# A share of the last weight block of a decode kernel is loaded ahead by a transfer of four by eight rows

## The chip, the cores and the metric

The kernel runs on one core of a Trainium2 chip. The metric is the device time of one execution in microseconds (us); the runs shown are compared by their median. All data is float32.

## The reference

Eight tokens (one for each of eight sequences) pass through an attention block that reads a key and value cache and, beside it, through a dense block; both results are added to the input.

```python
xn = _layernorm(x)                                    # x: 8 x 512
q  = xn @ wq                                          # 32 heads of 128, wq: 512 x 4096
scores = einsum("bhqd,bhkd->bhqk", q, k) * 128 ** -0.5   # 8 kv heads, 8192 keys, 4 q heads share one
p  = softmax(scores)
o  = einsum("bhqk,bhkd->bhqd", p, v)
A  = o.reshape(8, 4096) @ wo                          # wo: 4096 x 512
B  = mish(xn @ w1 + b1) @ w2                          # w1: 512 x 1792, w2: 1792 x 512
out = x + A + B
```

The key cache and the value cache have 268 MB each; everything else together is some 24 MB. So nearly all of the time goes into moving about 561 MB from memory into the core.

## The kernel before, in words

**Tiling and stages.** The work is cut into 16 packs (`PACKS`): four pairs of kv heads (`PAIRS`) by four pairs of sequences (`NP`, `PB`). Of each pack the loop takes two halves `b`. One half's keys or values are one transfer of 8 MB to all 128 partitions (64 KB a partition). For a half, `scores` (L353) multiplies the keys by the queries in 16 steps `r` of four TensorE passes each, `rows` (L365), `maximum`, `exponents`, `fold` and `weights` make the softmax's weights, and a round later `values` (L460) multiplies them by the values; `gather` (L471, L473) and `merge` (L488, L492) leave the head outputs `oT`. After a pair of heads is complete, `turn` (L514 to L528) brings `oT` into the layout in which `wo` lies, as `oW`, by four products with a selection matrix `tid` and four copies of 32 partitions, and `outputs` multiplies it by that pair's 2 MB of `wo`. `wo` lies so that partition p holds four rows of 1024 numbers (two head halves h by 512 output columns), 16 KB in all.

**Loads.** All big loads go through one queue, that of SP (L121), in one fixed order: the list `queue`, which `plan_k`, `plan_v`, `plan_wq`, `plan_wo` and the plan of `w2` fill ahead of time. Three places in the core's memory take them: `a` (64 KB a partition), `b` (80 KB a partition, so that two key loads overlap only in part) and `w` (16 KB a partition). `pump` issues the next load of the list as soon as its place is free, and `release` says that a place is free; the issue itself then waits on SP for the last instructions that read the bytes which it overwrites. SP takes its instructions in order, so a waiting load holds back all that stand behind it.

**The tail.** Behind the last pack, the order of the list is: the values of half 0 into `b`, the values of half 1 into `a` in two parts (three quarters and one quarter), and then `w2` in four parts (two, two, two and one of seven rows of 4 KB a partition) with the two halves of the last `wo` between them, as w2 0, w2 1, wo half 0, w2 2, wo half 1, w2 3. TensorE, VectorE and GpSimd run their instructions in program order. On TensorE the tail is: `values(0)`, `sums`, `merge(p, 0)`, `add_up` (L548), four idle products `keep_busy(4)` (L639) whose result nobody reads, `values(1)` in two parts, `down` (L628) with w2 0, `merge(p, 1)`, `turn`, `down` with w2 1, `last_outputs` (L562) with wo half 0, one idle product, `down` with w2 2, one idle product, `last_outputs` with wo half 1, and `down` with w2 3. Then VectorE copies the result out of the accumulator `H` (L720) and SP stores it (L721).

Of the kernel before, what the change touches and what calls it, by code (L numbers as in the profile page):

```python
# [8 lines left out]
F32 = mybir.dt.float32  # L9
AF = mybir.ActivationFunctionType  # L10
ALU = mybir.AluOpType
AX = mybir.AxisListType

P = 128
B = 8
# [8 lines left out]
G = 4  # L24
# [3 lines left out]
BW = 1024  # L28
# [4 lines left out]
Q = P // G  # L33
# [5 lines left out]
PAIRS = HKV // 2  # L39
# [11 lines left out]
KR = DH * 2 * NB // P  # L51
# [12 lines left out]

QR = CC
OR = 4
W1R = 2 * CC * P // P
W2R = G * FT // 2 * FP // P
FAR = 1e38
# [3 lines left out]
def kernel(  # L73
# [12 lines left out]
    nc = tc.nc  # L86
# [12 lines left out]
    def rows_of(blocks):  # L99

        return blocks.rearrange("j p f -> (j p f)").rearrange("(p f) -> p f", p=P)
# [12 lines left out]
    def plan(what, at, blocks, parts=((0, 1),), lo=0):  # L114

        rows = rows_of(blocks)
        n = rows.shape[1]
        t = place[at][:, lo : lo + n]

        def load(cols):  # L120
            nc.sync.dma_start(t[:, cols], rows[:, cols])  # L121
            return t

        for first, end in parts:
            cols = slice(round(first * n), round(end * n))
            queue.append((what, at, lambda cols=cols: load(cols)))
# [24 lines left out]
    def plan_v(p, b, at, parts=((0, 1),)):  # L151
        plan(("v", p, b), at, blocks_of(v, p, b), parts)
# [1 line left out]
    def plan_wq(i):  # L154
        plan(("wq", i), "w", wq[i * CC : (i + 1) * CC])

    def plan_wo(i, parts=((0, 1),)):
        plan(("wo", i), "w", wo[i * 4 : i * 4 + 4], parts)


    plan_wq(0)
# [5 lines left out]
    for p in range(PACKS):  # L167
        for b in range(PB):
# [4 lines left out]
            if p > 0:  # L173
                plan_v(p - 1, b, "a")
    plan_v(PACKS - 1, 0, "b")
    plan_v(PACKS - 1, 1, "a", ((0, 3 / 4), (3 / 4, 1)))
    W2_PARTS = ((0, 2), (2, 4), (4, 6), (6, 7))
    for k, (lo, hi) in enumerate(W2_PARTS):
        plan("w2", "b", w2, ((lo / W2R, hi / W2R),))
        if 0 < k < 3:  # L180
            plan_wo(PAIRS - 1, (((k - 1) / 2, k / 2),))


    S = psum.tile([P, GK], F32, name="s")
# [18 lines left out]
    hsel = const.tile([P, V8], F32, name="hsel")  # L203

    isel = const.tile([P, W4], F32, name="isel")

    far = const.tile([P, KINDS], F32, name="far")

# [15 lines left out]
    def setup():  # L224
        make_identity(nc, ident)
        nc.gpsimd.memset(ones, 1.0)
        nc.vector.memset(xnT, 0.0)
        nc.vector.memset(O[0], 0.0)

        st = const.tile([B, 8], F32, name="st")  # L230

        scratch = pt.rearrange("p b c m t e h -> p (b c m t e h)")
        xc, sq = scratch[:B, :D], scratch[:B, D : 2 * D]
        nc.vector.reduce_sum(st[:, 0:1], x_sb, axis=AX.X)
        nc.vector.tensor_scalar_mul(st[:, 1:2], st[:, 0:1], 1.0 / D)
        nc.vector.tensor_scalar(xc, x_sb, st[:, 1:2], None, op0=ALU.subtract)
        nc.vector.tensor_mul(sq, xc, xc)
        nc.vector.reduce_sum(st[:, 2:3], sq, axis=AX.X)
        nc.vector.tensor_scalar(
            st[:, 3:4], st[:, 2:3], 1.0 / D, EPS, op0=ALU.mult, op1=ALU.add  # L240
        )
        nc.scalar.activation(st[:, 4:5], st[:, 3:4], AF.Sqrt)
        nc.vector.reciprocal(st[:, 5:6], st[:, 4:5])

        nc.vector.tensor_mul(st[:, 6:7], st[:, 5:6], st[:, 5:6])
        nc.vector.tensor_mul(st[:, 7:8], st[:, 6:7], st[:, 3:4])
        nc.vector.tensor_scalar(st[:, 6:7], st[:, 7:8], -0.5, 1.5, op0=ALU.mult, op1=ALU.add)
        nc.vector.tensor_mul(st[:, 4:5], st[:, 6:7], st[:, 5:6])
        nc.vector.tensor_scalar(xc, xc, st[:, 4:5], None, op0=ALU.mult)
        for r in range(QR):  # L250
            nc.tensor.transpose(M[:, r * B : (r + 1) * B], xc[:, r::QR], ident[:B, :B])
        nc.vector.tensor_copy(
            xnT[:, :, :, :B],
            M[:, : QR * B]
            .rearrange("p (r o b) -> p r o b", r=QR, o=1)
            .to_broadcast([P, QR, 2, B]),
        )

        wide = scratch[:B, 2 * D : 2 * D + W1R * P]
        for t in range(2):  # L260
            nc.gpsimd.tensor_copy(
                wide.rearrange("b (r c t i) -> b r c t i", r=W1R, c=CC, t=2)[:, :, :, t, :],
                xc.rearrange("b (c i r) -> b r c i", c=CC, r=W1R),
            )

        nc.vector.tensor_copy(
            gsel, ident[:G, :G].rearrange("p (g o) -> p g o", o=1).to_broadcast([G, G, B])
        )
        nc.vector.reduce_sum(bsel, ident.rearrange("p (u i) -> p u i", u=KN), axis=AX.X)
        nc.vector.reduce_sum(  # L270
            half, ident.rearrange("p (g t i) -> p t g i", g=G, t=2), axis=AX.XY
        )
        nc.vector.reduce_sum(rsel, ident.rearrange("p (g r) -> p r g", g=G), axis=AX.X)
        nc.vector.reduce_sum(hsel, rsel.rearrange("p (i r) -> p r i", i=W4), axis=AX.X)
        nc.vector.reduce_sum(isel, rsel.rearrange("p (i r) -> p i r", i=W4), axis=AX.X)
        nc.vector.tensor_scalar(far, isel, FAR, -FAR, op0=ALU.mult, op1=ALU.add)
        of_head = const.tile([P, 2, V8], F32, name="of_head")
        nc.vector.reduce_sum(
            of_head, ident.rearrange("p (e j r) -> p e r j", e=2, j=NB), axis=AX.X
        )  # L280
        nc.vector.tensor_copy(tsel, of_head.rearrange("p e (b h) -> p b e h", b=PB))
        nc.vector.memset(csel, 0.0)
        for c in range(2):
            rows = slice(HE * c, HE * (c + 1))
            for b in range(PB):
                nc.vector.tensor_copy(
                    csel[rows, b, :, b], ident[rows, rows].rearrange("p (u h) -> p u h", u=KN)
                )
        return wide
# [155 lines left out]
    def sums(p, lsel):  # L445
        n = PB * 2 * REP
        nc.tensor.matmul(M[:, 136 : 136 + n], ones, lsel, start=True, stop=True)
        RT[p] = work.tile([P, PB, 2, REP], F32, name="r")
        nc.vector.reciprocal(RT[p].rearrange("p b e h -> p (b e h)"), M[:, 136 : 136 + n])
# [45 lines left out]
                RT.pop(p).rearrange("p b e h -> p (e h) b"),  # L495
            )

    def turning():

        tid = work.tile([P, HT * KINDS * P], F32, name="e", bufs=1)[:, : OR * P]  # L500
        tid = tid.rearrange("p (r g i) -> p r g i", r=OR, g=G)
        nc.vector.tensor_copy(
            tid, ident.rearrange("p (i r o) -> p r o i", r=OR, o=1).to_broadcast([P, OR, G, Q])
        )
        return tid

    def turn(i, tid):


        to = oW[i] = work.tile([P, OR, 2, B], F32, name="oW")  # L510
        o = oT.pop(i).rearrange("p n h b -> p (n h b)")
        cols = 2 * REP * B
        for r in range(OR):
            nc.tensor.matmul(  # L514
                M[:, 256 + r * cols : 256 + (r + 1) * cols],
                tid[:, r].rearrange("p g i -> p (g i)"),
                o,
                start=True,
                stop=True,
            )  # L520
        m = M[:, 256 : 256 + OR * cols].rearrange("p (r j q) -> p j r q", r=OR, j=G)
        for j in range(G):
            rows = slice(Q * j, Q * (j + 1))
            dst = to[rows].rearrange("p r h b -> p r (h b)")
            if i == PAIRS - 1 and j % 2:
                nc.scalar.copy(dst, m[rows, j])
            else:
                nc.vector.tensor_copy(dst, m[rows, j])  # L528
# [24 lines left out]
                stop=False,  # L553
            )

    def last_outputs(lo, hi, w):

        for r in range(lo, hi):
            for h in range(2):
                for g in range(G):  # L560
                    at = r * BW + h * D + g * P
                    nc.tensor.matmul(  # L562
                        H[Q * g : Q * g + B, :P],
                        oW[PAIRS - 1][:, r, h, :],
                        w[:, at : at + P],
                        start=False,
                        stop=False,
                    )
# [67 lines left out]
    def keep_busy(n):  # L636

        for k in range(n):
            nc.tensor.matmul(C[0][:Q, :], ones[:, :Q], acc, start=True, stop=True)  # L639
# [54 lines left out]

    p = PACKS - 1
    merges()
    tid = turning()
    values(0, landed["v", p, 0])
    gather(p, 0)
    release(("v", p, 0))  # L700
    sums(p, lsel.pop(p))
    merge(p, 0)
    add_up()
    keep_busy(4)
    values(1, landed["v", p, 1], 0, ROUNDS * 3 // 4)
    values(1, landed["v", p, 1], ROUNDS * 3 // 4)
    gather(p, 1)
    w2_sb, wo_sb = landed["w2"], landed["wo", PAIRS - 1]
    down(*W2_PARTS[0], w2_sb)
    merge(p, 1)  # L710
    turn(PAIRS - 1, tid)
    down(*W2_PARTS[1], w2_sb)
    last_outputs(0, OR // 2, wo_sb)
    keep_busy(1)
    down(*W2_PARTS[2], w2_sb)
    keep_busy(1)
    last_outputs(OR // 2, OR, wo_sb)
    down(*W2_PARTS[3], w2_sb)
    res = acc[:, :P]
    nc.vector.tensor_copy(res, H[:, :P])  # L720
# [58 lines left out]
```

## Time and profile before

| what | value |
|---|---|
| median of 3 runs | 1311.45 us (1311.45 to 1311.66) |
| the profiled execution | 1311.78 us |
| its span, first to last instruction | 1310.0 us |
| TensorE busy (matmul) | 863.7 us, 66% |
| VectorE busy | 384.0 us, 29% |
| ScalarE busy | 111.7 us, 9% |
| DMA | 561.76 MB, mean 429 GB/s |
| granted TensorE clock, mean | 0.844 |

How to read the profile: a line such as "1305.18 1.06 PE L562 MATMUL h<-kvw,oW 128*8 128x128 f32 x32 [0.56 <-DMA kvw<-in_wo]" says that at 1305.18 us from the span's start TensorE began 32 matmul passes of line 562 that took 1.06 us together, and that it had sat idle for 0.56 us before until a transfer from `wo` to place `w` landed. A float32 product takes two passes. "PEld" is the weight load of a pass. In the stretches, a DMA share of 1.00 means that all 16 DMA engines were moving packets all the time.

### The profile page before, as it was taken

The numbers are of one execution on the slowest core, as the hardware profiler recorded it, in microseconds if no ns is written. First come the engines' busy times: TensorE is split into PE (matmuls) and PEld (weight loads), VectorE is DVE, ScalarE is ACT, GpSimd is POOL, SyncE is SP. The second block draws the span as 40 slices with busy tenths as digits, with TensorE's granted clock in tenths as the row PEclk, the third lists the DMA queues.
The fourth block names the chain that finished last, engine by engine and source line by source line (L and its number), as shares of the span: only waits on it lengthen the run. The fifth ranks groups of instructions, "written<-read, shape, count | busy, mean of one in ns | idle before, by whom it ended". The sixth has DMA issues, their size and how long they took to land.

```text
span 1310.0 us, 10715 instructions
## 1 busy us (share of the span) xinstructions
PE 863.7 (66%) x4776; PEld 281.5 (21%) x4776; DVE 384.0 (29%) x590; ACT 111.7 (9%) x294; POOL 4.8 (0%) x10
## 2 busy tenths in 40 slices
PE   4786556866557765677565686655875666766657
PEld 1221112212112221122111222111221221222113
DVE  7150504205051230521405032052320505114051
ACT  1020101001010100101101010010100101001010
POOL 1000000000000000000000000000000000000000
PEclk9887889878799877898878897788877879878789
DMA  9999999999999999999999999999999999999997
GB/s 404 442 423 441 433 429 430 434 437 429 438 431 431 431 439 427 439 423 441 421 444 423 419 447 431 435 427 437 423 425 434 429 439 423 439 431 435 439 425 331
DMA packets 11591, 561.76 MB, mean 429 GB/s; under 512 B 1293, under 2 KB 1425, under 8 KB 1561
## 3 DMA queue, kind: packets, MB, share of 16 engines
q1 hardware_dynamic: 11520, 561.06, 99.3%
q8 instruction: 37, 0.61, 0.2%
q14 instruction: 10, 0.07, 0.0%
q10 hardware_dynamic: 24, 0.02, 0.0%
HBM read 561.01 MB, written 0.07 MB: 428 GB/s over the span
## 4 chain that ended last, share of the span: by engine, by line
DMA 67%; PE 32%; DVE 1%; issue 0%; SPq 0%; ACT 0%; ACTq 0%
DMA kvb<-in_kT 60%; PE c L353 30%; DMA kva<-in_kT 3%; DMA kvb<-in_w 2%; DMA kvb<-in_v 2%; PE o L581 0%; PE h L312 0%; PE o L460 0%; DMA sc<-in_x 0%; SPq L121 0%; DVE nm L379 0%; PE s L365 0%; DVE qT L340 0%; PE m L293 0%; PE o L575 0%
## 5 line engine op out<-in xcount | busy, mean ns | idle before, releaser
L353 PE MATMUL c<-kvb,qT 128*64 128x512 f32 x1984 | 502.4, 671 | 347.3 <-DMA kvb<-in_kT 345.7
L353 PEld LDWEIGHTS c<-kvb,qT 128*64 128x64 f32 x1984 | 162.0, 155 | 687.6 <-issue 470.4
L460 PE MATMUL o<-kva,pt 128*32 128x512 f32 x1984 | 231.4, 620 | 24.2 <-DMA kva<-in_v 24.2
L379 DVE TENSOR_REDUCE nm<-s 128x1 f32<-128x1024 f32 x16 | 19.6, 1225 | 462.2 <-PE s L365 462.2
L412 DVE STREAM_TRANSPOSE raw<-e 128x2048 f32<-128x2048 f32 x32 | 116.0, 3626 | 14.4 <-ACT e L404 12.7
L360 ACT COPY sc<-c 128x512 f32<-128x512 f32 x32 | 18.8, 586 | 1005.0 <-PE c L353 1005.0
L460 PEld LDWEIGHTS o<-kva,pt 128*32 128x32 f32 x1984 | 65.7, 113 | 179.3 <-issue 136.2
L404 ACT ACTIVATE e<-s,nms 128x512 f32<-128x512 f32 x128 | 86.3, 686 | 126.1 <-DVE nms L393 66.8
L492 DVE TENSOR_TENSOR oT<-m,r 128x16 f32<-128x16 f32 x16 | 2.8, 175 | 229.6 <-PE m L488 229.6
L471 DVE TENSOR_SCALAR os<-o,isel 128x128 f32<-128x128 f32 x32 | 11.1, 348 | 155.4 <-PE o L460 155.4
L430 DVE TENSOR_TENSOR pt<-raw 64x256 f32<-64x256 f32 x128 | 53.6, 418 | 2.0
L365 PE MATMUL s<-sc,csel 64*128 64x512 f32 x128 | 36.1, 641 | 8.4 <-ACT sc L360 8.4
L421 DVE TENSOR_TENSOR raw<-raw 128x1024 f32<-128x1024 f32 x32 | 39.2, 1225 | 1.1
L340 DVE TENSOR_TENSOR qT<-qc,bsel 128x1024 f32<-128x1024 f32 x32 | 37.6, 1218 | 0.0
L473 DVE SCALAR_TENSOR_TENSOR os<-o,isel,os 128x128 f32<-128x128 f32 x96 | 33.7, 351 | 3.4
L404 ACT ACTIVATION_READ_ACCUMULATOR e<-s,nms 128x1 f32 x128 | 26.0, 203 | 0.0
L380 PE MATMUL m<-ident,nm 128*1 128x128 f32 x16 | 4.3, 270 | 21.2 <-DVE nm L379 21.2
L312 PE MATMUL h<-kvw,xnT 128*64 128x512 f32 x64 | 16.2, 654 | 0.0
L488 PEld LDWEIGHTS m<-hsel,os 128*128 128x128 f32 x64 | 9.5, 188 | 29.6 <-issue 23.5
L488 PE MATMUL m<-hsel,os 128*128 128x8 f32 x64 | 12.4, 266 | 4.8 <-DVE os L473 3.3
L353 PE MATMUL c<-kva,qT 128*64 128x512 f32 x64 | 14.0, 593 | 1.6 <-DMA kva<-in_kT 1.6
L323 DVE TENSOR_SCALAR e<-h 128x512 f32<-128x512 f32 x16 | 9.9, 684 | 15.9 <-PE h L312 15.9
(100 smaller groups left out, 171.4 us busy)
## 6 DMA issues: line engine op xcount, KB each, us to landing
kvw<-in_wq SPq DMA_DIRECT2D x4, 2048.0 KB, 29.7
kvw<-in_wo SPq DMA_DIRECT2D x3, 2048.0 KB, 30.7
kva<-in_v SPq DMA_DIRECT2D x1, 6144.0 KB, 27.2
kva<-in_w SPq DMA_DIRECT2D x1, 3584.0 KB, 15.8
kvb<-in_w SPq DMA_DIRECT2D x3, 1024.0 KB, 20.6
kva<-in_v SPq DMA_DIRECT2D x1, 2048.0 KB
kvw<-in_wo SPq DMA_DIRECT2D x2, 1024.0 KB, 24.6
kvb<-in_w SPq DMA_DIRECT2D x1, 512.0 KB
```

The lines of the kernel that those rows point to most:

```text
L340: nc.vector.tensor_mul(qT[:, b], qc[:, k * PB + b] .rearrange("p r (o h) -> p r o h", o=1) .to_broadcast([P, KR, KN, REP]), bsel.rearrange ...
L353: nc.tensor.matmul(C[b][HE * c : HE * (c + 1), :], t[:, r], k[:, r * BW + c * 512 : r * BW + (c + 1) * 512], start=(r == order[0]), stop=( ...
L360: nc.scalar.copy(sc, C[b])
L365: nc.tensor.matmul(S[:, c * 512 : (c + 1) * 512], csel[HE * c : HE * (c + 1), b].rearrange("p u b h -> p (u b h)"), sc[HE * c : HE * (c + ...
L379: nc.vector.tensor_reduce(nm, S, axis=AX.X, op=ALU.max, negate=True)
L404: nc.scalar.activation(ex[:, :, s, :], S[:, c * 512 : (c + 1) * 512].rearrange("p (t f) -> p t f", t=HT), AF.Exp, bias=NMS[p][:, s : s + 1 ...
L412: nc.vector.transpose(raw.rearrange("p (m t r) -> p t m r", m=TW, t=HT), ex.rearrange("p t s (q m) -> p t m (s q)", m=TW),)
L421: nc.vector.tensor_add(raw[:, :, :n], raw[:, :, :n], raw[:, :, n:])
L430: nc.vector.tensor_add(pt[rows, b, c].rearrange("p m t e h -> p (m t) e h")[:, :, e], raw[rows, :, at : at + REP], raw[rows, :, V8 + at : ...
L460: nc.tensor.matmul(O[b][Q * c : Q * (c + 1), :], pt[:, b, j % 2, j // 2].rearrange("p t e h -> p (t e h)"), vt[:, W4 * DH * j : W4 * DH * ...
L473: nc.vector.scalar_tensor_tensor(os, O[b][:, DH * i : DH * (i + 1)], isel[:, i : i + 1], os, op0=ALU.mult, op1=ALU.add,)
L488: nc.tensor.matmul(M[:, at : at + 2 * REP], OS.pop((p, b)), hsel, start=True, stop=True)
```

## The change

The last 2 MB of `wo` (`last_wo`, 128 partition rows of 16 KB) are cut in another way.

- **Far part.** The second half (8 KB, its steps r = 2 and 3) of every fourth row (rows 3, 7, 11 and so on, 32 of them, 256 KB) comes by a transfer of its own, `plan_wo_far`. It stands in the list right behind the values of half 0 and goes to partitions 0 to 31 of place `b`, behind the columns that those values take (`OX_AT`). Its source is written as four by eight rows.
- **Near part.** What is left (1792 KB) comes by three transfers into place `w`, `plan_wo_near`: the even rows whole (64 rows), rows 1, 5, 9 and so on whole (32), and rows 3, 7, 11 and so on up to their half (32). They stand together between w2 1 and w2 2; before them GpSimd clears the second half of place `w`, because the bytes that the far part left out are still multiplied, by zeros.
- **TensorE and VectorE.** `turning` makes a second selection matrix `tif` for the far rows and clears their columns in `tid`. `turn` gets two more products, into `S`, and four more VectorE instructions that pick the far part of `oW` out of them. `last_outputs` runs twice: with the far part (half of the products that the whole block takes) between w2 1 and w2 2, and with the whole near part behind it. One idle product is dropped, and four of the others are split into two and two around `merge(p, 0)` and `add_up`.

```diff
+QS = 4
+QN = P // (QS * 2 * G)
+OH = OR // 2
...
+    OX_AT = KR * BW
+    last_wo = rows_of(wo[(PAIRS - 1) * 4 :])
+    def plan_wo_far():
+        half = last_wo.shape[1] // 2
+        t = place["b"][:Q, OX_AT : OX_AT + half]
+        rows = last_wo.rearrange("(a e s) f -> s e a f", e=QN, s=QS)[QS - 1]
+        def load():
+            nc.sync.dma_start(t, rows[:, :, half:])
+            return t
+        queue.append(("wo far", "behind b", load))
+    def plan_wo_near():
+        n = last_wo.shape[1]
+        t = place["w"][:, :n]
+        what = "wo", PAIRS - 1
+        def load(first, step, cols):
+            nc.sync.dma_start(t[first::step, :cols], last_wo[first::step, :cols])
+            return t
+        queue.append((what, "w", lambda: nc.gpsimd.memset(t[:, n // 2 :], 0.0)))
+        for first, step, cols in ((0, 2, n), (1, 4, n), (3, 4, n // 2)):
+            queue.append((what, "w", lambda a=(first, step, cols): load(*a)))
...
     plan_v(PACKS - 1, 0, "b")
+    plan_wo_far()
     plan_v(PACKS - 1, 1, "a", ((0, 3 / 4), (3 / 4, 1)))
...
-        if 0 < k < 3:
-            plan_wo(PAIRS - 1, (((k - 1) / 2, k / 2),))
+        if k == 1:
+            plan_wo_near()
...
+        nc.vector.reduce_sum(jsel, hsel.rearrange("p (j a) -> p j a", j=G), axis=AX.X)
...
+        if last:
+            own = tid[:, OH:, 0, QS - 1 :: QS].rearrange("p r (a e o) -> p a r e o", a=2, o=1)
+            for a in range(2):
+                nc.vector.tensor_copy(
+                    tif[:, :, :, :, a], own[:, a].to_broadcast([P, OR - OH, QN, G])
+                )
+            nc.vector.memset(tid[:, OH:, :, QS - 1 :: QS], 0.0)
...
+        if last:
+            for r in range(OR - OH):
+                nc.tensor.matmul(
+                    S[:Q, r * cols : (r + 1) * cols],
+                    tif[:, r].rearrange("p e j a -> p (e j a)"),
+                    o,
+                    start=True,
+                    stop=True,
+                )
...
+        if last:
+            m = S[:Q, : (OR - OH) * cols].rearrange("p (r j q) -> p j r q", j=G, q=2 * B)
+            dst = oW["far"].rearrange("p r h b -> p r (h b)")
+            nc.vector.tensor_scalar(dst, m[:, 0], jsel[:Q, 0:1], None, op0=ALU.mult)
+            for j in range(1, G):
+                nc.vector.scalar_tensor_tensor(
+                    dst, m[:, j], jsel[:Q, j : j + 1], dst, op0=ALU.mult, op1=ALU.add
+                )
...
     sums(p, lsel.pop(p))
+    keep_busy(2)
     merge(p, 0)
     add_up()
-    keep_busy(4)
+    keep_busy(2)
...
     down(*W2_PARTS[1], w2_sb)
-    last_outputs(0, OR // 2, wo_sb)
+    last_outputs(oW["far"], landed["wo far"])
     keep_busy(1)
+    last_outputs(oW[PAIRS - 1], wo_sb)
     down(*W2_PARTS[2], w2_sb)
-    keep_busy(1)
-    last_outputs(OR // 2, OR, wo_sb)
     down(*W2_PARTS[3], w2_sb)
```

More of the change, by code (lines that the diff above doesn't have):

```diff
@@ L155, in plan_wq, with plan_wo @@
         plan(("wq", i), "w", wq[i * CC : (i + 1) * CC])
-    def plan_wo(i, parts=((0, 1),)):
-        plan(("wo", i), "w", wo[i * 4 : i * 4 + 4], parts)
+    def plan_wo(i):
+        plan(("wo", i), "w", wo[i * 4 : i * 4 + 4])
+    OX_AT = KR * BW
[18 more added lines that the diff above has]
+            queue.append((what, "w", lambda a=(first, step, cols): load(*a)))
     plan_wq(0)
@@ L205 @@
     isel = const.tile([P, W4], F32, name="isel")
+    jsel = const.tile([P, G], F32, name="jsel")
     far = const.tile([P, KINDS], F32, name="far")
@@ L496, in merge, with turning @@
             )
-    def turning():
+    def turning(last=False):
         tid = work.tile([P, HT * KINDS * P], F32, name="e", bufs=1)[:, : OR * P]
@@ L504, in turning @@
         )
+        if last:
[5 more added lines that the diff above has]
+            nc.vector.memset(tid[:, OH:, :, QS - 1 :: QS], 0.0)
         return tid
     def turn(i, tid):
+        last = i == PAIRS - 1
         to = oW[i] = work.tile([P, OR, 2, B], F32, name="oW")
@@ L524, in turn @@
             dst = to[rows].rearrange("p r h b -> p r (h b)")
-            if i == PAIRS - 1 and j % 2:
+            if last and j % 2:
                 nc.scalar.copy(dst, m[rows, j])
@@ L554, in add_up, with last_outputs @@
             )
-    def last_outputs(lo, hi, w):
-        for r in range(lo, hi):
+    def last_outputs(o, w):
+        for r in range(o.shape[1]):
             for h in range(2):
@@ L563, in last_outputs @@
                         H[Q * g : Q * g + B, :P],
-                        oW[PAIRS - 1][:, r, h, :],
+                        o[:, r, h, :],
                         w[:, at : at + P],
@@ L696 @@
     merges()
-    tid = turning()
+    tif = qT.rearrange("p b r u h -> p (b r u h)")[:, : (OR - OH) * Q]
+    tif = tif.rearrange("p (r e j a) -> p r e j a", e=QN, j=G, a=2)
+    tid = turning(True)
     values(0, landed["v", p, 0])
@@ L710 @@
     merge(p, 1)
+    oW["far"] = sc[:Q, : (OR - OH) * 2 * B].rearrange("p (r h b) -> p r h b", h=2, b=B)
     turn(PAIRS - 1, tid)
     down(*W2_PARTS[1], w2_sb)
-    last_outputs(0, OR // 2, wo_sb)
+    last_outputs(oW["far"], landed["wo far"])
     keep_busy(1)
+    last_outputs(oW[PAIRS - 1], wo_sb)
     down(*W2_PARTS[2], w2_sb)
-    keep_busy(1)
-    last_outputs(OR // 2, OR, wo_sb)
     down(*W2_PARTS[3], w2_sb)
```

## The prediction

> **What bounds the kernel now.** I read the page's DMA queues and the shares of the chain that ended last, then TensorE's instructions at the end in order of time, then the DMA share of the last stretches.
>
> ```profile
> q1 hardware_dynamic: 11520, 561.06, 99.3%
> q8 instruction: 37, 0.61, 0.2%
> ...
> q10 hardware_dynamic: 24, 0.02, 0.0%
> ...
> DMA 67%; PE 32%; DVE 1%; issue 0%; SPq 0%; ACT 0%; ACTq 0%
> ...
> kvw<-in_wo SPq DMA_DIRECT2D x2, 1024.0 KB, 24.6
> kvb<-in_w SPq DMA_DIRECT2D x1, 512.0 KB
> ```
>
> Nearly all bytes go through SP's queue, and its packets keep the 16 engines 99.3% busy over the span. The kernel is bound by bytes per DMA engine; TensorE's 32% of the chain are products that a load waits for while the engines still move the one before. So an edit counts only if it changes when the last bytes land, or what follows them.
>
> TensorE's rows of the last 22 us:
>
> ```profile
> 1284.77 3.60 PE L639 MATMUL c<-acc,ones 128*32 128x512 f32 x8
> 1287.92 7.31 PE L460 MATMUL o<-kva,pt 128*32 128x512 f32 x64
> 1295.28 1.06 PE L628 MATMUL h<-kvb,aT 128*8 128x128 f32 x32
> 1296.88 0.39 PE L488 MATMUL m<-hsel,os 128*128 128x8 f32 x2 [0.54 <-DVE os L473]
> 1297.54 1.10 PE L514 MATMUL m<-oT,e 128*128 128x64 f32 x8 [0.27 <-DVE oT L492]
> 1298.57 1.06 PE L628 MATMUL h<-kvb,aT 128*8 128x128 f32 x32
> 1300.33 1.06 PE L562 MATMUL h<-kvw,oW 128*8 128x128 f32 x32 [0.70 <-DMA kvw<-in_wo]
> 1301.20 1.02 PE L639 MATMUL c<-acc,ones 128*32 128x512 f32 x2
> 1302.72 1.06 PE L628 MATMUL h<-kvb,aT 128*8 128x128 f32 x32 [0.50 <-DMA kvb<-in_w]
> 1303.60 1.02 PE L639 MATMUL c<-acc,ones 128*32 128x512 f32 x2
> 1305.18 1.06 PE L562 MATMUL h<-kvw,oW 128*8 128x128 f32 x32 [0.56 <-DMA kvw<-in_wo]
> 1306.43 0.62 PE L628 MATMUL h<-kvb,aT 128*8 128x128 f32 x16 [0.19 <-DMA kvb<-in_w]
> ```
>
> The last four loads land one behind the other, each with TensorE waiting: wo half 0 by 1300.33, w2 2 by 1302.72, wo half 1 by 1305.18, w2 3 by 1306.43. So 1024 KB take 1305.18 - 1302.72 = 2.46 us and 512 KB take 1.25 us, and the last landing sets the end.
>
> ```profile
> 1307.12 0.29 DVE L720 COPY acc<-h 128x128 f32<-128x128 f32 x1 [7.74 <-PE h L628]
> 1307.44 0.35 SPq L721 DMA_DIRECT2D out<-acc  x1
> ```
>
> Behind it lie 0.62 us of products, 0.29 of the copy, and the store; the change touches none of these.
>
> A load has landed when the latest of its engines is done. The stretches show that the engines don't end together:
>
> ```profile
> core 0: us, PE busy (x) PEld busy (x) DVE busy (x) ACT busy (x) POOL busy (x), PEclk, DMA share, GB/s
> 1301.00:1302.00 1.00, 1.00 (x18) 0.32 (x6) 0.00 (x0) 0.00 (x0) 0.00 (x0) 1.00 0.94 385
> 1302.00:1303.00 1.00, 0.50 (x13) 0.28 (x16) 0.00 (x0) 0.00 (x0) 0.00 (x0) 1.00 0.73 303
> 1303.00:1304.00 1.00, 1.00 (x32) 0.71 (x22) 0.00 (x0) 0.00 (x0) 0.00 (x0) 1.00 0.52 205
> 1304.00:1305.00 1.00, 0.62 (x2) 0.00 (x0) 0.00 (x0) 0.00 (x0) 0.00 (x0) 1.00 0.27 111
> 1305.00:1306.00 1.00, 0.81 (x32) 0.77 (x32) 0.00 (x0) 0.00 (x0) 0.00 (x0) 1.00 0.17 70
> ```
>
> Between 1303 and 1304 us a share of 0.52 means some eight engines at work, then four, then three. Half of the engines have nothing left some 2.5 to 3 us before the last landing. The five stretches lack 0.06 + 0.27 + 0.48 + 0.73 + 0.83 = 2.4 engine-shares times 1 us, so the same bytes dealt out perfectly would end 2.4 us earlier: no dealing of these bytes can gain more than that, 0.18%. A measurement of this kernel can tell about 0.2%, 2.6 us.
>
> **The near part, on the path: -0.6 us.** 256 KB of the last 2 MB no longer stand in the tail. At 2.46 us for 1024 KB, each engine has 256/1024 x 2.46 = 0.6 us less to do from there on, if the three near loads are spread over all 16 engines as evenly as the two halves were (64, 32 and 32 rows all divide by 16). Their 1792 KB take 1.75 x 2.46 = 4.3 us. From w2 1, which w2 2's wait puts at 1302.72 - 2 x 2.46 = 1297.8, near lands at 1302.1, w2 2 at 1304.6 and w2 3 at 1305.8. [...]
>
> **The far part, beside the path: 0.** The row for q10 tells how a load with few rows is dealt out: x has 8 rows and b1 has 4, and 24 packets are 12 rows and 12 completions, one engine to a row, where the 128-row loads of q1 have 80 x (128 + 16) = 11520 packets, 16 completions each. The far source leads with a dimension of four, so I take four engines. They move 64 KB each, what an engine moves of a 1024 KB load, 2.46 us, and save 0.6 like all others: 1.85 us later on four engines. That is nothing if they are among the eight that end by 1303.5 (then 1305.35, before 1305.8), and 1.85 us if one of them is among the late (second rival). Which engines are late no view tells. Following single packets through the trace by their times, as far as they can be told apart, the engines that took b1's rows are not among those that fetch instruction packets (q8), and it is these fetches, on half of the engines, that make engines late (0.2% of 16 engines' 1310 us for 37 packets, an estimate of 1.1 us each). So I take 0. [...]
>
> **SP's queue.** Far stands behind the values of half 0 and waits for two more steps of the last scores, ahead of the values of half 1.
>
> ```profile
> 1234.44 13.19 PE c L353 x48
> ```
>
> ```profile
> 1247.64 0.33 SPq L121 DMA_DIRECT2D kvb<-in_v  x1
> 1260.69 2.04 SPq L121 DMA_DIRECT2D kva<-in_v  x2
> ```
>
> The values issue after 48 of 64 passes, 12 of 16 steps; two steps more are 8 passes of 0.275 = 2.2 us, so far issues at about 1249.9, 10.8 us before the next load, which waits for its own buffer. One more near issue (0.33 to about 1 us) lies 20 us ahead of its bytes. With two loads more, w2 3 will have to wait on SP for a completion counter that the first part of half 1's values frees at 1287.9 (the row of L460), 13 us or more before its bytes move; only the store is behind it. All 0; had these covers gone, the price would be the wait itself.
>
> **GpSimd.** One clearing of 128x2048:
>
> ```profile
> 11.29 1.84 POOL L305 MEMSET pt<- 128x2048 f32 x1 [1.20 <-PE m L293]
> ```
>
> 1.84 us, from when the third wo has been used in pack 13, two packs ahead of the tail; nothing else stands in GpSimd's queue. 0.
>
> **VectorE and TensorE ahead of the tail.** `jsel` is one reduction among the setup's. `turning` gets two copies and a clearing, smaller than this one copy:
>
> ```profile
> 1273.86 0.61 DVE L502 COPY e<-ident 128x512 f32<-128x512 f32 x1
> 1282.50 0.35 DVE L471 TENSOR_SCALAR os<-o,isel 128x128 f32<-128x128 f32 x1 [8.03 <-PE o L460]
> 1282.88 1.12 DVE L473 SCALAR_TENSOR_TENSOR os<-o,isel,os 128x128 f32<-128x128 f32 x3
> ```
>
> under 1.8 us, with 8.03 us idle behind it: 0. The two idle products ahead of `merge` fill a wait for VectorE; two behind `add_up` instead of four end at 1284.77 + 1.8 = 1286.6, so TensorE idles 1.3 us before the values of half 1 at 1287.92. I take no loss of pace; the upper bound is
>
> ```profile
> 1273.46 8.97 PE L460 MATMUL o<-kvb,pt 128*32 128x512 f32 x64 [7.98 <-DMA kvb<-in_v]
> ```
>
> the same 64 passes after 7.98 us idle: 8.97 - 7.31 = 1.66 us (third rival).
>
> **TensorE's own path in the tail.** `turn` gets two products ahead of its four: 4 passes of 1.10/8, 0.55 us. Then `down` with w2 1 runs from 1299.1 to 1300.2. VectorE's four far instructions (at most 0.35 and 1.12, here on 32x32) take about 1 us from 1298.2 and so end at about 1299.2, when the four products of the near part are done too; the copies
>
> ```profile
> 1298.68 0.21 DVE L528 COPY oW<-m 32x64 f32<-32x64 f32 x1 [1.20 <-PE m L514]
> ...
> 1299.42 0.20 ACT L526 COPY oW<-m 32x64 f32<-32x64 f32 x1 [0.29 <-DVE oW L528]
> ```
>
> then take their 0.94 us, to 1300.2. `last_outputs` of far (half of 64 passes, 1.06) runs 1300.2 to 1301.3, the idle product (1.02) to 1302.3, near (64 passes, 2.12) to 1304.4, and then w2 2, landed at 1304.6, 1.06 to 1305.7, just before w2 3 lands at 1305.8. So TensorE stays ahead, by 0.1 to 0.2 us only.
>
> **Sum.** The profiled execution took 1311.78, 0.33 above the median. It becomes 1311.78 - 0.6 = 1311.2, its span 1309.4; against the median 1311.45, 1310.85.
>
> **Rivals.**
>
> First, on the other side, strided loads that run slower: the three near loads, each engine writing other partitions than in a 128-row load, get in each other's way. For it: all pace rows here are of 128-row loads. Against it: the three together spread over all partitions evenly. Price: any loss of pace in near falls on the end; 14% of its 4.3 us eats the gain, half the pace gives 1310.85 + 4.3 = 1315.1. [...]
>
> Second, the four far engines are among the late ones: where the latest of all is one, the last landing moves by +1.85 and the time is 1311.45 + 1.85 = 1313.3; a share of that where only a less late one is. Against it: half the engines end early, and the packets' trail above.
>
> Third, TensorE becomes the bound: 1.66 us lost in the values moves its whole tail, w2 3's products end at 1305.7 + 1.66 + 0.62 = 1308.0 instead of 1306.43 + 0.62 = 1307.05, and the time is 1311.45 + 0.95 = 1312.4. More than 0.1 to 0.2 us of delay begins to eat the gain, 0.8 turns it.
>
> Fourth, the change doesn't do what it says: far's 32 rows are dealt to all 16 engines, each moves as much as before, 1311.4.
>
> **How the numbers follow.** Forecast 0.52, first rival 0.20 (spread from 1310.9 to 1315.1), second 0.08, third 0.09, fourth 0.11. The forecast's own range is 1310.4 to 1311.2 (TensorE's thin margin; run-to-run spread 0.2). Range for all: 1310.2, a little under it, to 1313.6, where the upper half of the first rival is left out, 0.1. More than 2.6 us faster is barred by the 2.4 us of spare, 0.03 for what I don't see; slower than 1314.1 takes the first rival's upper part, 0.08, and 0.04 for the unseen.
>
> **What would show it.** Right: far on SP at about 1250; TensorE's wait for near ends by 1302.3, for w2 2 near 1304.6, for w2 3 near 1305.8; the DMA share of the last 3 us rises as four early engines work longer; copy L720's counterpart near 1306.5. Wrong: near lands later than 1302.5 (first rival), the last wait ends after 1306.4 with an otherwise unmoved near (second), no wait is left before w2 3's products (third), w2 3 lands at 1306.4 (fourth).

## The result, and the profile after

The changed kernel takes 1312.95 us, median of 22 runs (1312.37 to 1317.65), against 1311.43 us for the kernel before (22 runs). The ratio is 1.0015, with a 95% interval of 1.0008 to 1.0021: 1.5 us slower, where a gain of 0.6 us was forecast.

The profiled execution took 1316.36 us, 3.4 above the median, so a second profile of the same kernel (1315.02 us, 2.1 above the median of its own 11 runs) stands beside it below. No profile of a median run is there, so what follows shows where time is lost, and the medians how much. First the page of the changed kernel: the span, SP's queue (packets, MB, share of 16 engines' span) and the shares of the chain.

```profile
span 1314.5 us, 10800 instructions
...
q1 hardware_dynamic: 11444, 561.06, 99.2%
...
DMA 60%; PE 36%; DVE 3%; issue 0%; ACT 0%; ACTq 0%; DVEq 0%
```

The same bytes, the engines as busy as before. The packet count tells how the loads were dealt: 78 loads of 128 rows and 16 completions are 11232, the near loads add 64 + 16, 32 + 16 and 32 + 16, and what is left is 36, far's 32 rows and 4 completions. So far ran on four engines and the near loads on sixteen, as the prediction had it.

SP's queue of the changed kernel (start, length, line):

```profile
1248.95 0.81 SPq L174 DMA_DIRECT2D kvb<-in_wo  x1
1261.97 2.04 SPq L126 DMA_DIRECT2D kva<-in_v  x2
...
1282.70 10.59 SPq L126 DMA_DIRECT2D kvb<-in_w  x2
```

Far is issued at 1248.95, and the next load 13 us later. The last row holds the wait for a completion counter, which the trace puts down to the values in `a` (`kva<-in_v`, 9.7 us; their first part landed at 1292.90). It is over by 1293.3, some 10 us before the bytes behind it move.

TensorE's rows at the end, of the changed kernel:

```profile
1275.96 8.70 PE L496 MATMUL o<-kvb,pt 128*32 128x512 f32 x64 [10.31 <-DMA kvb<-in_v]
...
1287.28 1.88 PE L701 MATMUL c<-acc,ones 128*32 128x512 f32 x4
1292.94 8.74 PE L496 MATMUL o<-kva,pt 128*32 128x512 f32 x64 [3.78 <-DMA kva<-in_v]
1301.51 1.05 PE L690 MATMUL h<-kvb,aT 128*8 128x128 f32 x32
...
1308.28 1.80 PE L624 MATMUL h<-kvw,oW 128*8 128x128 f32 x57
...
1309.92 1.57 PE L690 MATMUL h<-kvb,aT 128*8 128x128 f32 x45
```

and of its second profile:

```profile
1291.77 7.07 PE L496 MATMUL o<-kva,pt 128*32 128x512 f32 x64 [2.05 <-DMA kva<-in_v]
1299.13 1.06 PE L690 MATMUL h<-kvb,aT 128*8 128x128 f32 x32 [0.29 <-DMA kvb<-in_w]
...
1305.94 1.94 PE L624 MATMUL h<-kvw,oW 128*8 128x128 f32 x64 [0.34 <-DMA kvw<-in_wo]
1308.34 1.06 PE L690 MATMUL h<-kvb,aT 128*8 128x128 f32 x32 [0.47 <-DMA kvb<-in_w]
1309.58 0.62 PE L690 MATMUL h<-kvb,aT 128*8 128x128 f32 x16 [0.18 <-DMA kvb<-in_w]
```

Read two distances. From the start of `values` of half 1 to the products with w2 3 it was 1306.43 - 1287.92 = 18.51 us before; in the second profile it is 1309.58 - 1291.77 = 17.81. So the tail did get shorter, by 0.7 us. But the values themselves, whose load TensorE waits for, start at 1292.94 and 1291.77 instead of 1287.92. The loss is ahead of the tail. Even the values of half 0, which stand ahead of far in the list, start 2.5 us later (1275.96, before 1273.46). Not all of the 5.0 and 3.85 us is the change's. The last pack's keys, long before far moves, already landed at 1235.04 and 1234.78 instead of 1234.39. And in the first profile one engine brings its share of the first part of half 1's values at 1292.90, when the other fifteen were done by 1291.22.

The stretches of 2 us while far moves, before:

```profile
core 0: us, PE busy (x) PEld busy (x) DVE busy (x) ACT busy (x) POOL busy (x), PEclk, DMA share, GB/s
1268.00:1270.00 2.00, 0.00 (x0) 0.00 (x0) 2.00 (x1) 0.00 (x0) 0.00 (x0) 0.50 0.99 426
1270.00:1272.00 2.00, 0.00 (x0) 0.00 (x0) 1.93 (x3) 0.00 (x0) 0.00 (x0) 0.50 0.95 410
1272.00:1274.00 2.00, 0.54 (x4) 0.23 (x8) 1.89 (x8) 0.00 (x0) 0.00 (x0) 0.50 0.91 393
1274.00:1276.00 2.00, 2.00 (x13) 0.46 (x9) 0.47 (x1) 0.00 (x0) 0.00 (x0) 0.50 1.02 442
```

and in the changed kernel:

```profile
1268.00:1270.00 2.00, 0.00 (x0) 0.00 (x0) 2.00 (x1) 0.00 (x0) 0.00 (x0) 0.76 0.98 348
1270.00:1272.00 2.00, 0.00 (x0) 0.00 (x0) 1.93 (x3) 0.00 (x0) 0.00 (x0) 0.50 0.81 205
1272.00:1274.00 2.00, 0.00 (x0) 0.00 (x0) 1.89 (x7) 0.00 (x0) 0.00 (x0) 0.50 0.98 246
1274.00:1276.00 2.00, 0.04 (x4) 0.07 (x7) 1.01 (x6) 0.00 (x0) 0.00 (x0) 0.50 1.05 365
```

The view counts a packet whole in the stretch in which it begins, so a share can be over 1 and neighbouring stretches trade some bytes. The DMA share hardly falls while the bytes per second fall by half: the engines are busy, but each packet takes longer. The four stretches move 2 us x (426 + 410 + 393 + 442) = 3.34 MB before and 2 us x (348 + 205 + 246 + 365) = 2.33 MB after. The missing 1.01 MB are 2.4 us at 427 GB/s, the mean of the changed kernel's page; in the second profile the same stretches lack 0.92 MB, 2.1 us. The records of single packets say the same. Far's packets of 8 KB begin at 0.31 us and soon take 0.50 to 0.70 us, most of them. The packets of the values of half 1 that other engines move meanwhile, 48 KB each, take 2.0 to 3.4 us instead of 1.8. The last ones of half 0, 64 KB each, take up to 4.25 us instead of 2.4, which is why these values too are late.

```
far's packets on its four engines, ns each (records of the changed kernel, followed by their times)
309 394 666 642 655 513 526 656
338 339 501 651 604 505 528 571
327 433 624 644 651 511 562 620
518 600 587 364 345 393 702 695
```

### The profile page after: what moved, and what is told of

Same layout as the page of the kernel before. It is cut to its first block, busy times and chain, and to the rows that moved or that the text cites. A ratio compares the mean times of both kernels' runs of the same rounds, so it can differ in the third digit from the quotient of the medians.

```text
span 1314.5 us, 10800 instructions
## 1 busy us (share of the span) xinstructions
PE 879.6 (67%) x4810; PEld 283.1 (22%) x4810; DVE 385.6 (29%) x598; ACT 111.6 (8%) x294; POOL 6.6 (1%) x11
## 3 DMA queue, kind: packets, MB, share of 16 engines
q1 hardware_dynamic: 11444, 561.06, 99.2%
## 4 chain that ended last, share of the span: by engine, by line
DMA 60%; PE 36%; DVE 3%; issue 0%; ACT 0%; ACTq 0%; DVEq 0%
DMA kvb<-in_kT 55%; PE c L389 31%; PE o L496 3%; DMA kva<-in_kT 2%; DMA kva<-in_v 2%; DVE raw L448 1%; DVE pt L466 0%; PE h L348 0%; PE o L643 0%; DVE nm L415 0%; PE s L401 0%; DVE os L509 0%; PE h L624 0%; DVE raw L457 0%; PE h L690 0%
## 5 line engine op out<-in xcount | busy, mean ns | idle before, releaser
L496 PE MATMUL o<-kva,pt 128*32 128x512 f32 x1984 | 242.1, 644 | 27.1 <-DMA kva<-in_v 27.1
L401 PE MATMUL s<-sc,csel 64*128 64x512 f32 x128 | 39.0, 688 | 8.1 <-ACT sc L396 8.1
L496 PE MATMUL o<-kvb,pt 128*32 128x512 f32 x64 | 8.7, 704 | 10.3 <-DMA kvb<-in_v 10.3
```

The source lines that it names most:

```text
L401: nc.tensor.matmul(S[:, c * 512 : (c + 1) * 512], csel[HE * c : HE * (c + 1), b].rearrange("p u b h -> p (u b h)"), sc[HE * c : HE * (c + ...
L496: nc.tensor.matmul(O[b][Q * c : Q * (c + 1), :], pt[:, b, j % 2, j // 2].rearrange("p t e h -> p (t e h)"), vt[:, W4 * DH * j : W4 * DH * ...
```

## The experiments

All are edits of the changed kernel. Times are medians of 11 runs; the kernel before stood at 1311.41, 1311.47 and 1311.41 in the three groups of runs (e0 to e3, e4 to e7, e8 to e10), and ratios are against it.

### Is it far at all?

The changed kernel once more, and without the issue of far:

```diff
-            nc.sync.dma_start(t, rows[:, :, half:])
             return t
```

> The changed kernel once more, for a second profile and for the comparison on this chip. All theories: 1312.5 to 1313.5 us. In the profile shown first the far load moved at about 0.5 to 0.65 us per 8 KB packet instead of 0.31, and packets of all other engines were longer while it ran, some 2.4 us times 16 engines in all. Theory S (source: the 32 far rows lie 64 KB apart in memory, so that four engines read the same small slice of every 64 KB): the same loss is here again, some 2 to 2.5 us of the whole DMA rate between 1268 and 1278 us. Theory P (place: four engines write partitions 0 to 31, the places of eight engines): the same. Theory T (TensorE's own tail is the bound): the last wait for a load is gone, TensorE runs without a gap to its end.

> The far transfer alone is left out: the far products run on what lies in its place, so that 256 KB of wo are missing from the result; all else is as changed. Theories S and P: the loss is the far transfer's, so the forecast of the near part comes true, 1310.6 to 1311.0 us, 0.5 to 0.9 under the kernel before. Theory T: 1312.3 or more, as TensorE's instructions are the same; a value between would share the loss out.

Measured: 1312.93 us for the kernel unchanged (ratio 1.0011, 1.0002 to 1.0020), 1311.05 without far (0.9996, 0.9987 to 1.0005). Far costs 1.9 us, so theory T, by which the time would stay, falls. Without far the stretches keep their rate:

```profile
1268.00:1270.00 2.00, 0.00 (x0) 0.00 (x0) 2.00 (x1) 0.00 (x0) 0.00 (x0) 0.50 0.93 401
1270.00:1272.00 2.00, 0.00 (x0) 0.00 (x0) 1.97 (x2) 0.00 (x0) 0.00 (x0) 0.50 1.00 434
1272.00:1274.00 2.00, 0.35 (x4) 0.23 (x8) 1.90 (x6) 0.00 (x0) 0.00 (x0) 0.50 0.91 393
1274.00:1276.00 2.00, 2.00 (x12) 0.45 (x8) 1.26 (x7) 0.00 (x0) 0.00 (x0) 0.50 0.97 418
```

What is left, the near part alone, is 0.4 us under the kernel before, a little less than expected, and its interval reaches over one. The near loads' own packets are not slowed (8 KB in 0.31 us and 16 KB in 0.61 in the changed kernel), so their alternate rows lose nothing, and 256 KB beside other work cost more than they save. The profiled execution of this run took 1312.98 us, 1.9 above its median.

### The source: its pitch, and the number of engines

Far's rows lie 64 KB apart in memory. One kernel reads 32 neighbouring rows (16 KB apart), the other reads far's own rows with a source whose leading dimension is 32; both write partitions 0 to 31.

```diff
 e2
-        rows = last_wo.rearrange("(a e s) f -> s e a f", e=QN, s=QS)[QS - 1]
+        rows = last_wo[:Q].rearrange("(e a) f -> e a f", e=QN)
 e3
-        rows = last_wo.rearrange("(a e s) f -> s e a f", e=QN, s=QS)[QS - 1]
+        rows = last_wo.rearrange("(x s) f -> s x f", s=QS)[QS - 1]
-            nc.sync.dma_start(t, rows[:, :, half:])
+            nc.sync.dma_start(t, rows[:, half:])
```

> The far transfer takes the second halves of the first 32 rows, which lie 16 KB apart, instead of every fourth row's, 64 KB apart; still four engines with eight rows each, the same 256 KB to the same partitions 0 to 31 (the numbers are the wrong rows', so the result is not the reference's). Theory S: the loss is gone, far's packets take 0.31 to 0.35 us, the DMA rate stays over 400 GB/s from 1268 to 1278 us, and the time is 1310.7 to 1311.3. Theory P: far's packets still take 0.5 to 0.65 us and the time stays at 1312.5 to 1313.5. Theory T: 1312.3 or more.

> The same 32 rows, 64 KB apart, and the same partitions 0 to 31, but the source written as 32 rows, so that 16 engines take two rows each (in another order of partitions, so the result is not the reference's). Theory S: reading is still from one slice of every 64 KB, the loss in DMA rate stays or is sharper and shorter, and the time is 1312 to 1313.5. Theory P: twice as many engines as places, the loss stays too, up to 1313.5. If instead it was the load of 64 KB on each of four engines that made them last: every engine moves as much as before, 1311.4 to 1311.8.

Measured: 1314.03 (1.0020, 1.0011 to 1.0029) and 1314.03 (1.0019, 1.0010 to 1.0028). In e2 the queue's packets are 11456, 48 for far instead of 36: 32 rows and 16 completions. So it too ran on sixteen engines, not on four as its expectation had it; its two leading dimensions are neighbours in memory and may have been taken as one. The two then differ in the pitch alone, and under this loss it makes no difference, so theory S falls. Nor is it the four engines: with sixteen the loss is no smaller, and both times lie above every range that was expected. What all of these have in common is the destination, 32 neighbouring partitions.

### The destination

The same load by four engines to every fourth partition (e4), the same to partitions 64 to 95 (e5), and the load by sixteen engines to every fourth partition (e7):

```diff
 e4
-            nc.sync.dma_start(t, rows[:, :, half:])
+            nc.sync.dma_start(place["b"][0::QS, OX_AT : OX_AT + half], rows[:, :, half:])
 e5
+            nc.sync.dma_start(place["b"][2 * Q : 3 * Q, OX_AT : OX_AT + half], rows[:, :, half:])
 e7 (source as in e3)
+            nc.sync.dma_start(place["b"][QS - 1 :: QS, OX_AT : OX_AT + half], rows[:, half:])
```

In e6 far is cut into two transfers of four by four rows, to partitions 0 to 15 and 32 to 47:

```diff
-            nc.sync.dma_start(t, rows[:, :, half:])
+            for c in range(2):
+                to = place["b"][2 * Q * c // 2 : 2 * Q * c // 2 + Q // 2, OX_AT : OX_AT + half]
+                nc.sync.dma_start(to, rows[:, QN * c : QN * (c + 1), half:])
```

> The same four engines and the same rows, but written to every fourth partition of all 128 instead of partitions 0 to 31 (so the far products run on other bytes and the result is not the reference's). Theory P1 (32 neighbouring partitions are too few places to write to, and what waits there holds back all engines): the loss is gone, the DMA rate stays over 390 GB/s from 1268 to 1278 us, far's packets take 0.31 to 0.36 us, 1310.8 to 1311.3 us. Theory P2 (an engine that writes partitions which in a 128-row load belong to another engine blocks that one): each of the four still writes into eight other engines' places, the loss stays, 1312.5 to 1313.5. Theory U (any load on few rows at this place in the queue costs this): 1312.5 to 1313.5.

> The same four engines and rows, written to partitions 64 to 95 (again not the reference's result). Theories P1, P2 and U: the loss is as with partitions 0 to 31, 1312.5 to 1314. If it mattered that the early engines' own partitions were hit, and not the late ones', it would be worse than the changed kernel by 0.5 us or more.

> [...] Theory P2: the loss is gone, far's packets take 0.31 us, 1310.8 to 1311.3 us. [...] Theory U: 1312.5 to 1314.

> The same 32 rows by 16 engines, written to the same partitions that the rows have in the source, every fourth of 128 (the far products run on other bytes, so not the reference's result). Theory P1: the loss is gone; every engine moves what it moved before the change, so 1311.4 to 1311.8 us, 0.6 over the kernel without the far transfer. Theories P2 and U: the loss stays as with 16 engines and partitions 0 to 31, 1313.5 to 1314.5.

Measured: e4 1312.72 (1.0009, 1.0001 to 1.0018), e5 1314.00 (1.0021, 1.0012 to 1.0030), e6 1310.74 (0.9993, 0.9984 to 1.0002), e7 1311.42 (0.9998, 0.9989 to 1.0007). With sixteen engines the destination decides: partitions 0 to 31 cost 2.6 us more (e3, 1314.03) than every fourth partition (e7), where all of far's packets take 0.31 to 0.32 us. With four engines, spreading the rows over all partitions heals little (e4, packets of about 0.5 us), and partitions 64 to 95 are 1.0 us worse than 0 to 31 (e5), more than the 0.5 us that its expectation gave for the case that it matters whose partitions are hit. Cutting the load into two, to partitions 0 to 15 and 32 to 47, heals all of it: the packets of e6 stay at 0.31 to 0.32 us, and its stretches read

```profile
1268.00:1270.00 2.00, 0.00 (x0) 0.00 (x0) 2.00 (x1) 0.00 (x0) 0.00 (x0) 0.50 0.85 369
1270.00:1272.00 2.00, 0.00 (x0) 0.00 (x0) 1.93 (x3) 0.00 (x0) 0.00 (x0) 0.50 0.92 393
1272.00:1274.00 2.00, 1.06 (x8) 0.46 (x12) 1.90 (x7) 0.00 (x0) 0.00 (x0) 0.50 1.02 442
1274.00:1276.00 2.00, 2.00 (x15) 0.45 (x8) 0.76 (x4) 0.00 (x0) 0.00 (x0) 0.50 1.08 467
```

or 3.34 MB, as before the change. TensorE's tail in e6:

```profile
1287.64 7.07 PE L498 MATMUL o<-kva,pt 128*32 128x512 f32 x64 [0.92 <-DMA kva<-in_v]
...
1302.00 1.94 PE L626 MATMUL h<-kvw,oW 128*8 128x128 f32 x64 [0.54 <-DMA kvw<-in_wo]
1304.25 1.06 PE L692 MATMUL h<-kvb,aT 128*8 128x128 f32 x32 [0.31 <-DMA kvb<-in_w]
1305.48 0.62 PE L692 MATMUL h<-kvb,aT 128*8 128x128 f32 x16 [0.17 <-DMA kvb<-in_w]
```

These are the landings that the prediction gave for near, w2 2 and w2 3 (1302.1, 1304.6, 1305.8), each some 0.1 to 0.35 us earlier. e7 stands where the fourth rival stood: on sixteen engines far saves nothing, and there it also costs nothing.

Of the theories on record, U (any load on few rows) falls with e6 and e7. P1 (too few places) is right in e7 and wrong in e4; what it says of e6 hangs on how many partitions make one place, which no run shows. P2 (engines that write other engines' partitions) is right in e4 and e6 (e5 tells none of the three apart), but it expected the loss to stay in e7, 1313.5 to 1314.5, and 1311.42 was measured. P2 can hold there only if the sixteen engines were dealt partitions of their own. Which partitions are an engine's own, and so how many engines' places a load hits, is an assumption in both P and P2: which engine wrote which partition no view shows.

### The same load, sixteen partitions further on

e6 differs from the changed kernel in two things, two transfers and other partitions. e9 is e6 with the partitions moved on by 16:

```diff
-                to = place["b"][2 * Q * c // 2 : 2 * Q * c // 2 + Q // 2, OX_AT : OX_AT + half]
+                to = place["b"][Q * c + Q // 2 : Q * c + Q, OX_AT : OX_AT + half]
```

> [...] Theory P2: the loss is back, packets of 0.45 to 0.65 us and 1312.5 to 1314 us. If only the count or the spread of places mattered, or the cut into two transfers was what helped: 1310.6 to 1311.2 as before.

Measured: 1313.79 (1.0023, 1.0014 to 1.0032), 3.05 us above e6. Source, sizes, number of transfers and the 32 partitions from the one to the other are those of e6, but most of the packets take 0.62 to 0.67 us and the rate falls:

```profile
1268.00:1270.00 2.00, 0.00 (x0) 0.00 (x0) 2.00 (x1) 0.00 (x0) 0.00 (x0) 0.50 1.11 299
1270.00:1272.00 2.00, 0.00 (x0) 0.00 (x0) 1.92 (x4) 0.00 (x0) 0.00 (x0) 0.50 0.98 221
1272.00:1274.00 2.00, 0.00 (x0) 0.00 (x0) 1.91 (x7) 0.00 (x0) 0.00 (x0) 0.50 0.93 238
1274.00:1276.00 2.00, 0.03 (x4) 0.06 (x5) 0.53 (x4) 0.00 (x0) 0.00 (x0) 0.50 0.95 397
```

So what counts is which partitions the load writes, and neither the cut into two nor the count of partitions, 32 in both. P2's range for e9, 1312.5 to 1314, holds the 1313.79. But that the four engines write 0 to 15 and 32 to 47 in a 128-row load too, and other engines write 16 to 31 and 48 to 63, was the author's assumption: no view of these runs shows the engines' numbers or their partitions. With far on four engines the times are 1310.74 (e6), 1312.72 (e4), 1312.93 (e0, partitions 0 to 31), 1313.79 (e9) and 1314.00 (e5), and why they stand in this order is not shown.

### The change with the loss taken out

e8 is e6 with the selection matrix and the picks of VectorE laid out for 48 partitions (16 of them zeros between the two blocks), so that it computes the whole reference. e10 takes the second halves of every second row instead of every fourth: 512 KB, two transfers of eight by four rows on eight engines, to partitions 0 to 31 and 32 to 63.

```diff
 e8
+QF = Q + QN * G
...
-            nc.sync.dma_start(t, rows[:, :, half:])
+            for c in range(2):
+                to = place["b"][Q * c : Q * c + QN * G, OX_AT : OX_AT + half]
+                nc.sync.dma_start(to, rows[:, G * c : G * (c + 1), half:])
...
 e10, beside that
-QS = 4
+QS = 2
...
-        for first, step, cols in ((0, 2, n), (1, 4, n), (3, 4, n // 2)):
+        for first, step, cols in ((0, 2, n), (1, 2, n // 2)):
```

> The changed kernel with its far part written as in the run with partitions 0 to 15 and 32 to 47, and the far products laid out for these partitions (48 of them, 16 with zeros), so that the result is the reference's. Theory P2 (an engine that writes partitions which belong to another engine in a 128-row load costs all of them): no loss, 1310.6 to 1311.0 us, what the forecast had. If the far products had been helped by reading other bytes there: up to 1311.5.

> [...] The result is the reference's. Theory P2, with the spare of the eight early engines taken from the stretches: the tail is 512/1024 x 2.46 = 1.23 us shorter and the early engines 1.23 us longer, 1310.0 to 1310.5 us. If the eight engines are not the early ones, or TensorE becomes the bound: 1310.8 to 1312.7.

Measured: e8 1310.87 us (1310.58 to 1312.28; ratio 0.9994, 0.9985 to 1.0002), e10 1313.12 (1311.03 to 1313.30; 1.0008, 0.9999 to 1.0017). e8 is 0.54 below the kernel before and 2.1 below the changed kernel; of 11 runs nine are under 1311.2, but the interval just reaches one, so the gain over the kernel before is not clear of the noise. That the loss is gone is: e9, in the same group of runs, stands 2.9 us higher. The tail of e8:

```profile
1287.24 7.07 PE L504 MATMUL o<-kva,pt 128*32 128x512 f32 x64 [1.57 <-DMA kva<-in_v]
...
1305.21 0.62 PE L701 MATMUL h<-kvb,aT 128*8 128x128 f32 x16 [0.19 <-DMA kvb<-in_w]
```

17.97 us between the two, 0.54 under the 18.51 of before. e10 is above both ranges that were expected for it. No packet of its far part is slow (0.309 to 0.319 us), although one of its two transfers goes to the partitions 0 to 31 of the changed kernel, on eight engines by the count of its packets (11472, 80 for far). On four and on sixteen engines these partitions cost over 1.5 us, on eight far's packets and the 48 KB packets beside them (1.83 us at most) keep their time. So it is not the place as such that costs. Which engines write it, and how many, differs between these runs, and nothing here tells the two apart. Yet the end is late:

```profile
1290.56 7.07 PE L504 MATMUL o<-kva,pt 128*32 128x512 f32 x64 [2.02 <-DMA kva<-in_v]
...
1306.53 1.06 PE L701 MATMUL h<-kvb,aT 128*8 128x128 f32 x32 [0.36 <-DMA kvb<-in_w]
1307.77 0.62 PE L701 MATMUL h<-kvb,aT 128*8 128x128 f32 x16 [0.18 <-DMA kvb<-in_w]
```

The tail itself is 17.21 us, 1.30 under the 18.51 of before (forecast 1.23). The values of half 1 start 2.6 us late, though. Their first part lands on fifteen engines by 1289.32 and on the last at 1290.52, and the last load by 1306.55 and at 1307.73. As far as its packets can be followed, that engine is one of the eight of far. That is the second rival, with eight engines instead of four. One profile doesn't tell how often it happens, and its keys already landed 0.9 us later than in the kernel before (1235.27 against 1234.39), which the runs don't explain.

## Why the prediction was wrong, by its own steps

**What bounds the kernel** held: the same 561.06 MB keep the engines at 99.2%, and the end moves with the last landing.

**The near part, on the path: -0.6 us** held. Its three loads land by 4.30 us after w2 1 in both profiles of the changed kernel (forecast 4.3, by the latest engine of each load in the trace). The time from the start of half 1's values to w2 3's products fell by 0.70 us (second profile), 0.67 (e6) and 0.54 (e8). In e1's profile it rose, to 18.90; there one engine lands each late load 1.05 us behind the rest (w2 3 at 1307.40, the others by 1306.35). In medians the gain was 0.36 without far (e1), 0.73 (e6) and 0.54 (e8), each with an interval that reaches one.

**The far part, beside the path: 0** is the step that failed. Its engine count was right (36 packets), and so was the weight of its bytes; what it left out is that far's packets and all others could get slower while far moves. The step took 2.46 us for 64 KB per engine from a 128-row load; in the changed kernel far's packets take 4.04 to 4.37 us on the four engines above, and the core moves 1.01 MB less in 8 us than before, worth 2.4 us (2.1 in the second profile). In medians far cost 1.9 us (1312.93 - 1311.05). The same bytes from the same rows on four engines cost nothing when the partitions were others (e6), so the step's value, 0, was right for a load that this change does not contain. The prediction had the doubt at hand, engines that write other partitions than in a 128-row load, but weighed it for the near part alone (first rival), where it did no harm.

**SP's queue, GpSimd** held: far at 1248.95 (forecast 1249.9), the wait for a counter over some 10 us before its bytes move (forecast 13 or more) and so off the path, the clearing 1.80 us at 1097.5 (forecast 1.84), and the tail of e6 and e8 is not held up.

**VectorE and TensorE ahead of the tail: 0.** Forecast was an idle time of 1.3 us ahead of the values; it was 3.78 and 2.05, since their load came late. With 2.05 the 64 passes took 7.07, with 3.78 they took 8.74. So the price of the third rival (1.66) came out as 1.67 us in one profile, as a consequence of the late load and not as its cause.

**TensorE's own path** held, where the loads are on time: in e6 it waits 0.54, 0.31 and 0.17 us for the last three. The estimate of 2.12 us for near's 64 passes measured 1.94, the four passes of `turn` 0.38 instead of 0.55. Only in the profile in which the values started after 3.78 us of idle time has TensorE no wait left.

**Sum and rivals.** The sum, 1310.85, is e8's time within 0.02, closer than its interval can tell, and the changed kernel's not: 1312.95 is 2.1 above it, inside the range but on the other side of the kernel before. First rival: loads that get in each other's way are what happened in another part, while far moves; that engines write other partitions there was the author's reason, and the runs show only that the partitions matter (e6 and e9, 3.05 us). At its place, the near loads, it fell: no run shows the half pace behind its 1315.1, near landed in 4.30 us. Second: in the changed kernel's first profile the last landing of every late load comes from one engine, 1.7 us behind the rest (1308.99 and 1310.72 for w2 3), one of far's as far as packets can be followed. So there far's engines were not all among the early ones. The prediction took them as early by the packets' trail of b1's rows; that far runs on the engines of those rows no run shows. In the second profile the last is 0.4 us behind (1309.10 and 1309.54). In the median this can be no more than a part, since e6 too runs far on four engines and has no such loss. Third: seen in one profile, above. Fourth: the packet count rules it out, and e7 shows its time, 1311.42.

Open: why the times of the changed kernel spread up to 1317.65, why e7 loses nothing, and why all sixteen engines slow down and not far's four alone.

## What to carry to other kernels

A load that is "beside the path" is only free if it leaves the other engines' rate alone: read the GB/s of the stretches in which it moves, not the DMA share, which stayed at 0.8 to 1.05 while the rate fell from 410 and 393 to 205 and 246 GB/s. When a load has fewer rows than partitions, try it with other destinations: cut in two as in e6, or some partitions further on. Sixteen partitions were worth 3 us here (e6 and e9). And before moving bytes to engines that end early, find out how firmly those engines are the early ones.

## What the runs showed of the hardware that was not expected

- 256 KB that four engines write to 32 neighbouring partitions cut the rate of all sixteen from 410 and 393 GB/s to 205 and 246; the same bytes to partitions 0 to 15 and 32 to 47 left it at 393 and 442, and to 16 to 31 and 48 to 63 brought it down to 221 and 238. The packets that other engines move meanwhile slowed as well (48 KB in 2.0 to 3.4 us instead of 1.8). Where on their way they are held up these runs do not show.
- A pitch of 64 KB or 16 KB between source rows of 8 KB made no difference in two runs that both carry this loss (1314.03 both).
- A source written as four by eight rows was dealt to sixteen engines where its two dimensions are neighbours in memory (e2, 48 packets), to four where they are not (36 packets).
